# A convolution by FFT in front of two feed-forward layers: filter tiles loaded in pairs and unfolded on ScalarE

## The chip, the cores and the metric

The kernel runs on one core of one Trainium2 chip. The metric is the device time of one execution in microseconds (us). A core has five engines that run side by side, each through its own list of instructions in order: TensorE (PE in the profile, its weight loads PEld), VectorE (DVE), ScalarE (ACT), GpSimd (POOL) and SyncE (SP), which only issues transfers. They wait for one another by semaphores.

## What is computed

The input x has 2 batches of 3008 rows and 256 columns. Each column is convolved with a filter by way of the Fourier transform, and the result goes through two feed-forward layers with 2048 hidden units:

```python
X = np.fft.rfft(x, axis=1)
Y = X * (filt_r + 1j * filt_i)[None, :, :]
x = np.fft.irfft(Y, n=x.shape[1], axis=1).reshape(B * S, D)
h = x @ moe_w_in
x = np.where(h > 0.0, h, np.exp(np.minimum(h, 0.0)) - 1.0) @ moe_w_out
h = x @ moe2_w_in
return (h * np.clip(h + 3.0, 0.0, 6.0) / 6.0) @ moe2_w_out
```

## The kernel before

The transform of 3008 points is split into 47 times 64. A batch is handled in two halves of 128 columns (h is 0 or 1). For each half the opening runs these stages, which the string `PROLOGUE` (line 865) names by letters, with the half and a number behind:

- S1 (`s1t`, line 154): the 47-point transforms, seven pieces of up to 5 rows. For half 0 they run before the string starts; the letter A is that stage for half 1. Each piece fills a PSUM bank and is copied into the tile `zt`, in turn by ScalarE and VectorE.
- T (`tr`, line 170): four transposes of `zt` into a bank and a copy of it into SBUF: by ScalarE for g 0, 2, 3, 4, 5, by VectorE for g 1. The first T of a half needs all seven copies of S1.
- S (`s2_mm` and `mult`, lines 210 and 217): the 64-point transforms of group g (6 groups in a half), then the product with the filter: VectorE makes two products of 64 partitions (the imaginary part, with the halves of the partitions exchanged) and one of 128 (the real part), GpSimd adds them.
- I (`i2_mm`, `i2_evac`): the inverse 64-point transform, a copy by ScalarE and a store to a scratch in DRAM (`scr2`) that regroups the rows.
- V and O (`v_load`, `i1_mm`, `i1_evac`): the scratch is loaded again and the inverse 47-point transforms run. V for a half needs all six stores of the half.

The filter tile of half h and group g holds on its 128 partitions the 64 frequencies twice over (the host doubles them, line 1196), the real part and the imaginary part side by side. `f_load` (line 142) loads one tile of 512 KB, `f_sign` (line 146; the letter F) multiplies its imaginary part on GpSimd by a sign table `sg`. There are 12 such tiles for batch 0, all loaded at the start, and 12 again for batch 1 much later (lines 993 and 994).

`LOADS` (line 872) gives the order in which SyncE issues the first transfers: F is a filter tile, X a quarter of the input of half 1, W the raw weights, M a matrix. The other letters of `PROLOGUE`: c and k take one step of the conversion of weights into two parts (`w_chain`, line 383 on), B runs S1 for batch 1, X splits a block for the first layer, G and H run the first matmuls of the first layer (`g1_half`, `g1`), x and w load input and weights. After the string, the loop over `units` (line 1095) runs the first layer, two or three steps of weight conversion beside each unit.

The order is written out by hand: inside `tc.manual_schedule()` every engine runs its instructions in the order in which the program makes them, and semaphores are put in from the data. PSUM has seven banks in a rotating pool (`bank`, line 55) and one alone; tiles of 4 KB per partition come from a pool of 21 (`t4`, line 53).

Of the kernel before, what the change touches and what calls it, by code (L numbers as in the profile page):

```python
# [9 lines left out]
F32 = mybir.dt.float32  # L10
# [13 lines left out]
P = 128  # L24
# [23 lines left out]
def fft_conv_moe_moe2(ctx, tc, xp, fq, sg, cs1, cs1t, cs2, ci2, ci1, ident, w1i, w1o, w2i, w2o, out):  # L48
# [16 lines left out]
    def t4(shape, dt=F32):  # L65
        return p4.tile(shape, dt, tag="t4", name=name("t4"))
# [10 lines left out]
    def evac(eng, dst, src):  # L77
        if eng is nc.scalar:
            nc.scalar.activation(dst, src, AF.Copy)
        else:  # L80
            eng.tensor_copy(dst, src)  # L81
# [10 lines left out]
    def flat(t):  # L92
        return t.rearrange("p k d -> p (k d)")
# [19 lines left out]
    def load_mat(key, src, queue=nc.scalar):  # L113
        k, m = src.shape
        mats[key] = const.tile([k, m], F32, name=key)
        queue.dma_start(mats[key], src)
# [19 lines left out]
    def x_load(b, h, q):  # L136
        xin[b, h, q] = t4([P, 8, P])
        n = 4 if (b, h, q) == (0, 0, 0) else 8
        for j in range(0, 8, n):
            nc.sync.dma_start(xin[b, h, q][:KP, j : j + n], xp[b, h, :, 8 * q + j : 8 * q + j + n, :])  # L140

    def f_load(b, h, g):
        filt[b, h, g] = t4([P, 2, 4, P])
        nc.sync.dma_start(filt[b, h, g], fq[h, g])

    def f_sign(b, h, g):
        fi = filt[b, h, g][:, 1, :, :]
        s = mats["sg"][:, 4 * g : 4 * g + 4].unsqueeze(2).broadcast_to([P, 4, P])
        nc.gpsimd.tensor_tensor(out=fi, in0=fi, in1=s, op=ALU.mult)


    zt = {}

    def s1t(b, h, jg, eng):
# [60 lines left out]
            mm3(accs[h, g], *mats["s2r"], *map(pairs, parts), True, True)  # L215

    def mult(b, h, g):
        f = filt.pop((b, h, g))
        acc, parted = accs.pop((h, g)), lambda t: t
        if b:  # L220
            acc, parted = sorted_(acc), halves_of
        u, v = t2([P, 512]), t2([P, 512])
        for c in range(2):
            a, o = slice(64 * c, 64 * c + 64), slice(64 - 64 * c, 128 - 64 * c)
            nc.vector.tensor_tensor(out=parted(v[o]), in0=acc[a], in1=parted(flat(f[a, 1])), op=ALU.mult)
        nc.vector.tensor_tensor(out=parted(u), in0=acc, in1=parted(flat(f[:, 0])), op=ALU.mult)
        ws[b, h, g] = t2([P, 512])
        nc.gpsimd.tensor_tensor(out=ws[b, h, g], in0=u, in1=v, op=ALU.add)  # L228

# [45 lines left out]
    def w_raw(layer, f):  # L275
        wi, wo = ((w1i, w1o), (w2i, w2o))[layer]
        raw = p4.tile([P, 512, 2], U32, tag="t4", name=name("raw"))
        nc.sync.dma_start(
            raw[:, 0:256, :].rearrange("p (c f) t -> p c (f t)", c=2),
            wi.bitcast(U32)[:, f * 2 * P : (f + 1) * 2 * P].rearrange("(c p) f -> p c f", p=P),  # L280
        )
        nc.sync.dma_start(
            raw[:, 256:512, :].rearrange("p f t -> p (f t)"),
            wo.bitcast(U32)[f * P : (f + 1) * P, :],
        )
        raws[layer, f] = raw
# [566 lines left out]
    def fetch1(f):  # L853
# [9 lines left out]


    PROLOGUE = """
        T00 T01 T02 S00 T03 F01 S01 T04 F01 S02 T05 F01 S03 I00 F01 S04 I01 F01 A10 A11 F01 S05
        I02 A12 A13 A14 I03 c01 F01 A15 A16 c01 I04 T10 c01 T11 I05 F01 T12 w00 x00 S10 T13 S11
        T14 F01 S12 T15 S13 V00 I10 F01 S14 I11 S15 k01 B00 I12 O00 I13 O01 I14 o02 c01 I15 c01
        c01 k01 c01 x01 O03 X00 X01 O04 V10 k01 O05 k01 k01 w01 O06 B01 G00 X02 G01 k01 B02 B03
        O10 o11 o12 G02 X10 X11 O13 k01 o14 X12 k01 k01 k01 H00 O15 k01 H01 k01 H02 O16  # L870
    """
    LOADS = [(0, None, q, None) for q in range(4)]
    for x in "F00 F01 F02 F03 X0 X1 X2 X3 F04 F05 F10 W0 M F11 F12 F13 F14 F15".split():
        if x == "M":
            LOADS.append((None, None, None, None))
        elif x[0] == "F":
            LOADS.append((int(x[1]), int(x[2]), None, None))
        elif x[0] == "W":
            LOADS.append((None, None, None, int(x[1:])))
        else:  # L880
            LOADS.append((1, None, int(x[1:]), None))
    conv = w_chain(WLEAD, NF, fetch1, True)
    n_steps = 7 * (NF - WLEAD) - 12
    span = NI * (NF - 1) - 1
# [137 lines left out]
        i1(1, jg, T + 43 + max(0, jg - 1))  # L1022

    with tc.manual_schedule():
        for key, src in (("s1t", cs1t), ("id", ident), ("sg", sg), ("s2", cs2), ("i2", ci2), ("i1", ci1)):
            load_mat(key, src)
        three = const.tile([P, 1], F32, name="three")
        nc.vector.memset(three, 3.0)
        engs = (nc.scalar, nc.vector)

        acc = bank()
        for n in WARM:
            zeros = (nc.const_aps.tensor(0.0, [P, k], F32) for k in (P, n))
            nc.tensor.matmul(acc[:, :n], *zeros, start=True, stop=True)  # L1034
        for h, g, q, r in LOADS:
            if q is not None:
                x_load(0, h, q)
            elif g is not None:
                f_load(0, h, g)
            elif r is not None:  # L1040
                w_raw(0, r)
            else:
                load_mat("s1", cs1, nc.sync)
        for jg in range(JG):
            s1t(0, 0, jg, engs[jg % 2])
        lead = w_chain(0, WLEAD, lambda f: None)
        f_sign(0, 0, 0)
        f_sign(0, 0, 1)
        nsign = 2
        for step in PROLOGUE.split():  # L1050
            what, h, g = step[:-2], int(step[-2]), int(step[-1])
            if what == "T":
                tr(0, h, g, nc.scalar if g > 1 else engs[g])
            elif what == "S":
                s2_mm(0, h, g)
                mult(0, h, g)
            elif what == "A":
                s1t(0, h, g, engs[g % 2])
            elif what == "I":
                i2_mm(0, h, g)  # L1060
                i2_evac(0, h, g)
            elif what == "V":
                for q in range(4):
                    v_load(0, h, q)
            elif what == "O":
                i1_mm(0, h, g)
                i1_evac(0, h, g, nc.scalar)
            elif what == "o":
                i1_mm(0, h, g)
                i1_evac(0, h, g, nc.vector)  # L1070
            elif what == "k":
                steps(conv, g)
            elif what == "c":
                steps(lead, g)
            elif what == "X":
                x_split(0, g, h)
            elif what == "F":
                for _ in range(g):
                    f_sign(0, *divmod(nsign, 6))
                    nsign += 1  # L1080
            elif what == "x":
                x_load(1, h, g)
            elif what == "w":
                w_raw(0, WLEAD + g)
            elif what == "B":
                s1_plain(h, g)
                s1_evac(1, h, g, True)
            elif what == "G":
                g1_half(units[g], 0)
            elif what == "H":  # L1090
                g1(units[g])
                if g:
                    g_split(units[g - 1])

        for n, u in enumerate(units):
            place[0] = n
            for fn in pre[n]:
                fn()
            if n >= NI:
                g1(u)  # L1100
                g_split(units[n - 1])
            if n >= SKEW:
                g2(units[n - SKEW])
            for fn in post[n]:
                fn()
        def rest(n):
            def run():
                if n == NU:
                    g_split(units[-1])
                g2(units[n - SKEW])  # L1110
                for fn in post[n]:
                    fn()
            return run

        old = None
        n = place[0] = NU
        for l, p in ROUNDS:
            for q in range(GROUPS):
                old = group(l, p, q, old, [rest(NU + i) for i in range(3)], pre[n : n + 4])
                n += 4  # L1120
        prod(old.l, old.p, old.q, 3, old.c, False)
        old.high((1, 1))
        old.gate((1, 0))
        old.add((0, 1), old.u2, old.c)
        old.low((1, 1))
        old.high((1, 0))
        old.relu((0, 1))
        old.low((1, 0))
        old.gate((0, 1))
        old.high((0, 1))  # L1130
        old.low((0, 1))
        for key in ((0, 0), (1, 1), (1, 0), (0, 1)):
            old.second(key)
            if key == (1, 0):
                out_evac(old.l, old.p, 0)
        out_evac(old.l, old.p, 1, True)
# [82 lines left out]
```

## Time and profile before

| | before |
|---|---|
| median of 3 runs | 1045.99 us (1045.93 to 1046.16) |
| the profiled execution | 1045.9 us |
| its span in the trace | 1044.0 us |
| TensorE busy | 1037.5 us, 99% of the span |
| VectorE busy | 873.3 us, 84% |
| ScalarE busy | 805.8 us, 77% |
| GpSimd busy | 194.7 us, 19% |
| granted TensorE clock over the span | 1.00 |

The profile gives each engine's busy time as a share of the span. The 1.9 us between the span and the execution's time lie outside what the trace covers. TensorE's matmuls are pipelined and their ends are modelled, so its busy share hides short gaps; these are better read from the starts of its instructions.

### The profile page before, as it was taken

Reading aid. Unit: us, or ns where it says so; the run is one execution under the profiler, and the core shown is the slowest. Engines: PE = TensorE matmul, PEld = TensorE weight load, DVE = VectorE, ACT = ScalarE, POOL = GpSimd, SP = SyncE. Lnnn points to the kernel's source line nnn. Section 1 sums busy time; section 2 is a strip of 40 time slices with the busy share of each in tenths; the row PEclk is TensorE's granted clock in tenths of the full one; section 3 lists DMA queues with packets and bytes.
Section 4 is the critical chain, followed back from the end, with each engine's and each line's share of the span. In section 5 each row is a group of like instructions: output and inputs, shape, how many; then the busy total and the mean of one; then the engine's idle time right before and its main releaser. Section 6 shows DMA issues by size and latency. Waiting matters only on the chain.

```text
span 1044.0 us, 14383 instructions
## 1 busy us (share of the span) xinstructions
PE 1037.5 (99%) x5018; PEld 913.5 (88%) x5018; DVE 873.3 (84%) x1412; ACT 805.8 (77%) x1448; POOL 194.7 (19%) x212
## 2 busy tenths in 40 slices
PE   9999999999999999999999999999999999999998
PEld 6688888888899989988888888888888888888998
DVE  4889999888877788799898988888888888887776
ACT  3488888897778888888988877777777777777775
POOL 3700002455447735000111000010010010000000
PEclk9999999999999999999999999999999999999999
DMA  9992100475546534330385432100100100100101
GB/s 285 327 306 82 31 1 1 152 235 178 173 124 216 198 125 154 127 102 11 124 291 144 153 126 82 41 21 21 41 21 21 41 18 19 40 1 1 41 1 36
DMA packets 58056, 107.31 MB, mean 103 GB/s; under 512 B 5024, under 2 KB 33696, under 8 KB 57984
## 3 DMA queue, kind: packets, MB, share of 16 engines
q1 hardware_dynamic: 52112, 88.16, 25.4%
q0 software_dynamic: 4896, 17.83, 5.6%
q8 instruction: 39, 0.64, 0.3%
q10 hardware_dynamic: 976, 0.41, 0.2%
q14 instruction: 33, 0.27, 0.1%
HBM read 69.42 MB, written 36.96 MB: 102 GB/s over the span
## 4 chain that ended last, share of the span: by engine, by line
PE 97%; ACT 1%; DVE 1%; POOL 0%; issue 0%; DVEq 0%; ACTq 0%; POOLq 0%
PE ps L88 27%; PE ps L89 27%; PE ps L90 27%; PE lone L88 3%; PE lone L90 3%; PE lone L89 3%; PE ps L256 2%; PE ps L160 1%; PE ps L233 1%; PE ps L213 1%; PE ps L1034 0%; PE ps L173 0%; POOL t L228 0%; PE ps L184 0%; DVE t L85 0%
## 5 line engine op out<-in xcount | busy, mean ns | idle before, releaser
L88 PE MATMUL ps<-t,w 128*128 128x512 f32 (+1 forms) x1072 | 403.4, 376 | 0.7 <-DVE t L509 0.7
L89 PE MATMUL ps<-t,w 128*128 128x512 f32 (+1 forms) x1072 | 401.5, 375 | 0.0
L90 PE MATMUL ps<-t,w 128*128 128x512 f32 (+1 forms) x1072 | 401.4, 374 | 0.0
L88 PEld LDWEIGHTS ps<-t,w 128*128 128x128 f32 x1072 | 202.6, 189 | 25.5 <-DVE t L509 1.7
L89 PEld LDWEIGHTS ps<-t,w 128*128 128x128 f32 x1072 | 202.6, 189 | 24.7 <-DVE w L327 1.2
L90 PEld LDWEIGHTS ps<-t,w 128*128 128x128 f32 x1072 | 202.6, 189 | 24.0 <-DVE t L701 0.2
L701 DVE TENSOR_TENSOR t<-t,t 128x512 fp32r<-128x512 f32 (+1 forms) x256 | 175.6, 699 | 24.3 <-ACT t L696 22.7
L696 ACT ACTIVATE t<-t 128x512 fp32r<-128x512 f32 (+1 forms) x256 | 154.2, 616 | 6.0 <-DVE t L686 5.7
L650 ACT ACTIVATE t<-ps 128x512 f32<-128x512 f32 (+1 forms) x175 | 102.6, 586 | 60.6 <-PE ps L90 58.9
L670 ACT ACTIVATE t<-t,three 128x512 f32<-128x512 f32 (+1 forms) x143 | 96.5, 707 | 38.0 <-DVE t L656 37.2
L686 DVE SCALAR_TENSOR_TENSOR t<-t,t 128x512 f32<-128x512 f32 (+1 forms) x143 | 97.0, 705 | 33.3 <-ACT t L670 32.8
L506 ACT ACTIVATE t<-ps 128x512 f32<-128x512 f32 (+1 forms) x128 | 74.3, 581 | 45.1 <-PE ps L90 36.3
L656 DVE TENSOR_TENSOR t<-ps,t 128x512 f32<-128x512 f32 (+1 forms) x128 | 86.7, 678 | 11.4 <-ACT t L650 10.8
L507 ACT ACTIVATE t<-t 128x512 f32<-128x512 f32 (+1 forms) x128 | 79.3, 619 | 4.1
L509 DVE SCALAR_TENSOR_TENSOR ps<-t,ps 128x512 f32<-128x512 f32 (+1 forms) x76 | 50.4, 664 | 30.3 <-ACT t L507 29.6
L85 DVE TENSOR_TENSOR t<-t,t 128x512 fp32r<-128x512 f32 (+2 forms) x92 | 66.7, 730 | 3.7 <-ACT t L84 3.5
L84 ACT ACTIVATE t<-t 128x512 fp32r<-128x512 f32 (+2 forms) x104 | 62.8, 616 | 1.8 <-DVE t L81 1.3
L570 POOL TENSOR_TENSOR t<-t,t 128x512 f32<-128x512 f32 (+1 forms) x12 | 16.3, 1359 | 243.5 <-DVE t L656 214.4
L90 PE MATMUL ps<-t,t 128*128 128x512 f32 (+1 forms) x160 | 60.1, 376 | 0.0
L89 PE MATMUL ps<-t,t 128*128 128x512 f32 (+1 forms) x160 | 60.1, 376 | 0.0
L88 PE MATMUL ps<-t,t 128*128 128x512 f32 (+1 forms) x160 | 60.1, 376 | 0.0
L90 PE MATMUL lone<-t,w 128*128 128x512 f32 (+1 forms) x144 | 54.0, 375 | 0.0
(121 smaller groups left out, 1607.7 us busy)
## 6 DMA issues: line engine op xcount, KB each, us to landing
t<-in_fq SPq DMA_DIRECT2D x24, 512.0 KB, 6.2
scrw<-t SPq DMA_DIRECT2D x16, 512.0 KB, 3.0
w<-scrw POOLq DMA_DIRECT2D x16, 512.0 KB, 4.3
scr<-t SPq DMA_DIRECT2D x24, 256.0 KB, 3.3
t<-scr SPq DMA_DIRECT2D x16, 384.0 KB, 5.9
t<-in_xp SPq DMA_DIRECT2D x15, 384.0 KB, 6.2
scrx<-t SPq DMA_DIRECT2D x10, 512.0 KB, 3.1
t<-scr POOLq DMA_DIRECT2D x10, 512.0 KB, 4.8
```

Of the source, the lines that this page charges most:

```text
L85: eng.tensor_tensor(out=lo, in0=src, in1=_f32(hi), op=ALU.subtract)
L88: nc.tensor.matmul(acc, wh, xh, start=start, stop=False, skip_group_check=more)
L89: nc.tensor.matmul(acc, wl, xh, start=False, stop=False, skip_group_check=more)
L90: nc.tensor.matmul(acc, wh, xl, start=False, stop=stop, skip_group_check=more)
L506: nc.scalar.activation(r, acc, AF.Relu, scale=-1.0)
L507: nc.scalar.activation(t[:, :n], t[:, :n], AF.Exp, scale=-1.0)
L650: nc.scalar.activation(like(t, self.n), got(bank_, self.n), AF.Copy)
L656: nc.vector.tensor_tensor(out=like(self.h[key], n), in0=got(bank_, n), in1=like(u, n), op=ALU.add)
L670: nc.scalar.activation(like(r, n), h, AF.Relu, bias=three)
L686: stt(out=r, in0=r, scalar=6.0, in1=h, op0=ALU.min, op1=ALU.mult)
L696: nc.scalar.activation(gh[:, : self.n], g[:, : self.n], AF.Copy)
L701: nc.vector.tensor_tensor(out=gl[:, :n], in0=g[:, :n], in1=_f32(gh[:, :n]), op=ALU.subtract)
```

## The change

Two neighbouring groups of a half (2r and 2r + 1) share one transfer: the upper 64 partitions of the one and the lower 64 of the next lie side by side in DRAM, so 512 KB hold both filters once. `p_load` (the letter P in `LOADS`) issues it into a tile t. `f_even` (the letter d in `PROLOGUE`) puts the signs on both with one GpSimd instruction and has ScalarE make three copies of 64 partitions by 512 columns into a second tile u; after it group 2r can be used. `f_odd` (the letter e) makes two more copies, after which group 2r + 1 can be used. `mult` takes its halves from t and u accordingly. Further: the copies of S1 for half 1 (A) are all on ScalarE; the matrices `i2` and `i1` are loaded by SyncE's queue among the first loads, not by ScalarE's; a second sign table `pairsg` is made by two small GpSimd copies; `LOADS` and `PROLOGUE` have a new order. Batch 1 keeps `f_load` and `f_sign`.

```diff
+    def p_load(h, r):
+        filt[0, h, 2 * r] = t4([P, 2, 4, P])
+        rows = fq.rearrange("h g p c k d -> (h g p) (c k d)")
+        first = (6 * h + 2 * r) * P
+        nc.sync.dma_start(
+            filt[0, h, 2 * r].rearrange("p c k d -> p (c k d)"), rows[first + 64 : first + 64 + P]
+        )
+
+    lower, upper = slice(0, 64), slice(64, P)
+
+    def f_even(h, r):
+        t, u = filt[0, h, 2 * r], t4([P, 2, 4, P])
+        filt[0, h, 2 * r + 1] = u
+        nc.gpsimd.tensor_tensor(
+            out=t[:, 1], in0=t[:, 1],
+            in1=mats["pairsg"][:, r].unsqueeze(2).broadcast_to([P, 4, P]), op=ALU.mult,
+        )
+        evac(nc.scalar, u[lower, 0], t[lower, 0])
+        evac(nc.scalar, u[upper, 0], t[lower, 0])
+        nc.scalar.activation(u[upper, 1], t[lower, 1], AF.Copy, scale=-1.0)
+
+    def f_odd(h, r):
+        t, u = (filt[0, h, 2 * r + i] for i in range(2))
+        evac(nc.scalar, t[lower, 0], t[upper, 0])
+        nc.scalar.activation(u[lower, 1], t[upper, 1], AF.Copy, scale=-1.0)
@@ def mult(b, h, g):
-        f = filt.pop((b, h, g))
+        if b:
+            real = filt.pop((b, h, g))
+            imag = real, real
+        else:
+            t, u = (filt[b, h, g // 2 * 2 + i] for i in range(2))
+            real = t if g % 2 else u
+            imag = (u, t) if g % 2 else (t, u)
...
-            nc.vector.tensor_tensor(out=parted(v[o]), in0=acc[a], in1=parted(flat(f[a, 1])), op=ALU.mult)
-        nc.vector.tensor_tensor(out=parted(u), in0=acc, in1=parted(flat(f[:, 0])), op=ALU.mult)
+            nc.vector.tensor_tensor(out=parted(v[o]), in0=acc[a], in1=parted(flat(imag[c][a, 1])), op=ALU.mult)
+        nc.vector.tensor_tensor(out=parted(u), in0=acc, in1=parted(flat(real[:, 0])), op=ALU.mult)
@@ the order of the opening
-        T00 T01 T02 S00 T03 F01 S01 T04 F01 S02 T05 F01 S03 I00 F01 S04 I01 F01 A10 A11 F01 S05
-        I02 A12 A13 A14 I03 c01 F01 A15 A16 c01 I04 T10 c01 T11 I05 F01 T12 w00 x00 S10 T13 S11
-        T14 F01 S12 T15 S13 V00 I10 F01 S14 I11 S15 k01 B00 I12 O00 I13 O01 I14 o02 c01 I15 c01
-        c01 k01 c01 x01 O03 X00 X01 O04 V10 k01 O05 k01 k01 w01 O06 B01 G00 X02 G01 k01 B02 B03
-        O10 o11 o12 G02 X10 X11 O13 k01 o14 X12 k01 k01 k01 H00 O15 k01 H01 k01 H02 O16
+        x00 T00 d00 e00 T01 T02 T03 d01 S00 T04 S01 T05 c01 A10 A11 e01 x01 d02 S02 I00 c01 e02
+        w00 A12 d10 S03 I01 S04 I02 S05 A13 A14 I03 A15 A16 I04 c01 I05 w01 T10 e10 c01 c01 T11
+        d11 T12 S10 S11 V00 T13 T14 T15 k01 e11 B00 d12 S12 e12 S13 S14 I10 S15 I11 O00 I12 k01
+        I13 O01 I14 c01 X00 o02 I15 c01 B01 B02 k01 k01 X01 O03 k01 X02 k01 O04 k01 G00 k01 G01
+        k01 O05 G02 V10 k01 O06 k01 B03 k01 O10 o11 o12 k01 X10 X11 O13 o14 X12 H00 O15 H01 H02
+        O16
-    for x in "F00 F01 F02 F03 X0 X1 X2 X3 F04 F05 F10 W0 M F11 F12 F13 F14 F15".split():
+    LOADS = "P00 X0 i2 P01 W0 X1 P02 i1 X2 X3 P10 P11 P12 M".split()
@@ before the opening
-        for key, src in (("s1t", cs1t), ("id", ident), ("sg", sg), ("s2", cs2), ("i2", ci2), ("i1", ci1)):
+        for key, src in (("s1t", cs1t), ("id", ident), ("sg", sg), ("s2", cs2)):
             load_mat(key, src)
+        mats["pairsg"] = const.tile([P, 3, 4], F32, name="pairsg")
+        for i, half in enumerate((lower, upper)):
+            signs = mats["sg"].rearrange("p (r i k) -> p i r k", r=3, i=2)
+            nc.gpsimd.tensor_copy(mats["pairsg"][half], signs[half, i])
...
-        f_sign(0, 0, 0)
-        f_sign(0, 0, 1)
...
-                s1t(0, h, g, engs[g % 2])
+                s1t(0, h, g, nc.scalar)
```

## Rows read from the trace of the kernel before

**Rows 1.** The page's first part: engine, busy us (share of span), instructions.
```profile
PE 1037.5 (99%) x5018; PEld 913.5 (88%) x5018; DVE 873.3 (84%) x1412; ACT 805.8 (77%) x1448; POOL 194.7 (19%) x212
```

**Rows 2.** TensorE in order of time: start, us, instruction, count [idle before, releaser].
```profile
20.02 1.02 PE L233 MATMUL ps<-t,i 128*128 128x512 f32 x2
20.88 1.02 PE L213 MATMUL ps<-t,s 128*128 128x512 f32 x2
22.12 1.12 PE L233 MATMUL ps<-t,i 128*128 128x512 f32 x2 [0.21 <-POOL t L228]
...
33.81 1.04 PE L173 MATMUL ps<-id,zt 128*128 128x128 f32 x8
...
41.62 1.02 PE L213 MATMUL ps<-t,s 128*128 128x512 f32 x2
42.80 1.12 PE L233 MATMUL ps<-t,i 128*128 128x512 f32 x2 [0.16 <-POOL t L228]
...
51.64 1.13 PE L233 MATMUL ps<-t,i 128*128 128x512 f32 x2
...
56.83 0.78 PE L88 MATMUL ps<-t,w 128*128 128x512 f32 x1
57.45 0.38 PE L89 MATMUL ps<-t,w 128*128 128x512 f32 x1
57.67 0.38 PE L90 MATMUL ps<-t,w 128*128 128x512 f32 x1
...
59.82 0.59 PE L184 MATMUL ps<-t,s 96*96 96x512 f32 x1
60.55 3.56 PE L256 MATMUL ps<-i,t 96*128 96x94 f32 x30
...
71.88 0.38 PE L89 MATMUL lone<-t,w 128*128 128x512 f32 x1
72.28 0.48 PE L90 MATMUL lone<-t,w 128*128 128x512 f32 x1
72.60 0.38 PE L88 MATMUL ps<-t,w 128*128 128x512 f32 x1
...
78.21 0.38 PE L90 MATMUL ps<-t,w 128*128 128x512 f32 x1
79.32 0.48 PE L88 MATMUL ps<-t,w 128*128 128x512 f32 x1 [0.73 <-DVE t L509]
```

**Rows 3.** Busy us of each engine by stretch, then clock, DMA share and GB/s.
```profile
20.00:30.00 10.00, 9.79 (x57) 6.97 (x57) 8.63 (x13) 3.04 (x5) 9.30 (x9) 1.00 1.03 368
30.00:40.00 10.00, 10.00 (x57) 6.89 (x57) 8.04 (x13) 5.54 (x10) 5.62 (x6) 1.00 1.01 331
```

**Rows 4.** ScalarE in order of time, in the opening.
```profile
14.52 0.60 ACT L79 ACTIVATE t<-ps 128x512 f32<-128x512 f32 x1 [0.74 <-PE ps L173]
...
44.03 0.60 ACT L243 ACTIVATE t<-ps 128x512 f32<-128x512 f32 x1 [1.60 <-PE ps L233]
44.52 0.66 ACT L306 ACTIVATE t<-raw 128x512 f32<-128x512 f32 x1
...
54.40 1.15 ACT L84 ACTIVATE t<-t 128x512 fp32r<-128x512 f32 x2
```

**Rows 5.** VectorE in order of time: the products with the filters.
```profile
39.23 1.39 DVE L225 TENSOR_TENSOR t<-ps,t 64x512 f32<-64x512 f32 x2
...
41.37 1.39 DVE L225 TENSOR_TENSOR t<-ps,t 64x512 f32<-64x512 f32 x2
```

**Rows 6.** GpSimd in order of time: a sign and an addition.
```profile
19.80 1.04 POOL L149 TENSOR_TENSOR t<-t,sg 128x512 f32<-128x512 f32 x1
20.80 1.26 POOL L228 TENSOR_TENSOR t<-t,t 128x512 f32<-128x512 f32 x1
```

**Rows 7.** ScalarE in order of time, as the loop over units begins.
```profile
73.71 0.89 ACT L306 ACTIVATE t<-raw 128x512 f32<-128x512 f32 x1
74.51 0.58 ACT L506 ACTIVATE t<-ps 128x512 f32<-128x512 f32 x1
```

More of the change, by code (lines that the diff above doesn't have):

```diff
@@ L865, in fft_conv_moe_moe2 @@
     PROLOGUE = """
-        T00 T01 T02 S00 T03 F01 S01 T04 F01 S02 T05 F01 S03 I00 F01 S04 I01 F01 A10 A11 F01 S05
-        I02 A12 A13 A14 I03 c01 F01 A15 A16 c01 I04 T10 c01 T11 I05 F01 T12 w00 x00 S10 T13 S11
-        T14 F01 S12 T15 S13 V00 I10 F01 S14 I11 S15 k01 B00 I12 O00 I13 O01 I14 o02 c01 I15 c01
-        c01 k01 c01 x01 O03 X00 X01 O04 V10 k01 O05 k01 k01 w01 O06 B01 G00 X02 G01 k01 B02 B03
-        O10 o11 o12 G02 X10 X11 O13 k01 o14 X12 k01 k01 k01 H00 O15 k01 H01 k01 H02 O16
-    """
-    LOADS = [(0, None, q, None) for q in range(4)]
-    for x in "F00 F01 F02 F03 X0 X1 X2 X3 F04 F05 F10 W0 M F11 F12 F13 F14 F15".split():
[L874 to L881, printed above, removed]
+        x00 T00 d00 e00 T01 T02 T03 d01 S00 T04 S01 T05 c01 A10 A11 e01 x01 d02 S02 I00 c01 e02
[4 more added lines that the diff above has]
+        O16
+    """
+    LOADS = "P00 X0 i2 P01 W0 X1 P02 i1 X2 X3 P10 P11 P12 M".split()
     conv = w_chain(WLEAD, NF, fetch1, True)
@@ L1034, in fft_conv_moe_moe2 @@
             nc.tensor.matmul(acc[:, :n], *zeros, start=True, stop=True)
[L1035 to L1041, printed above, removed]
+        for q in range(4):
+            x_load(0, 0, q)
+        for x in LOADS:
+            n = int(x[-1]) if x[1:] else 0
+            if x[0] == "P":
+                p_load(int(x[1]), n)
+            elif x[0] == "X":
+                x_load(0, 1, n)
+            elif x[0] == "W":
+                w_raw(0, n)
+            elif x[0] == "i":
+                load_mat(x, {"i1": ci1, "i2": ci2}[x], nc.sync)
             else:
@@ L1046, in fft_conv_moe_moe2 @@
         lead = w_chain(0, WLEAD, lambda f: None)
-        f_sign(0, 0, 0)
-        f_sign(0, 0, 1)
-        nsign = 2
         for step in PROLOGUE.split():
@@ L1076, in fft_conv_moe_moe2 @@
                 x_split(0, g, h)
[L1077 to L1080, printed above, removed]
+            elif what == "d":
+                f_even(h, g)
+            elif what == "e":
+                f_odd(h, g)
             elif what == "x":
```

## The prediction

> **What bounds the kernel now.** I read the busy times first: TensorE is busy 1037.5 of 1044.0 us [rows 1]. The reader is to see that no edit of the opening can win more than the gaps of TensorE there; the matmuls themselves are the same before and after, only their order changes. Next I read the list of TensorE's instructions in order of time and subtract starts, since modelled ends hide gaps. Where nothing is waited for, two 512-column records of an S or I step take 20.88 - 20.02 = 0.86 us, and one record of the first layer takes 57.67 - 57.45 = 0.22 [rows 2]. Against these, six places in the first 80 us are late [rows 2]:
>
> - a. 20.88 to 22.12 is 1.24 instead of 0.86: 0.38, an I step waiting for GpSimd's addition.
> - b. 41.62 to 42.80 is 1.18: 0.32, the same in half 1.
> - c. 56.83 to 57.45 is 0.62 instead of 0.22: 0.40, the first matmul of the first layer (G00).
> - d. 59.82 to 60.55 is 0.73 instead of 0.43 (half of 0.86): 0.30, the first O step of half 1, whose load V has only just landed.
> - e. 71.88 to 72.60 is 0.72 for two records instead of 0.44: 0.28.
> - f. 78.21 to 79.32 is 1.11 instead of 0.22: 0.89, a bank not yet released by VectorE.
>
> Together 2.57 us. Some single waits of about 0.1 are left uncounted, and the wait before the first T stays as it is: the code up to it is the same.
>
> **The change part by part.** *Transfers.* Six loads of 512 KB fall away, 3.1 MB. The stretches 20 to 40 move 331 to 368 GB/s with the DMA engines at a share of 1.0 [rows 3], so that is some 9 us of a full queue. None of it is on TensorE's path as long as the data lands before its turn, and in list a to f only d waits for a transfer: V of half 1 stands in SyncE's queue behind an input load that the new order issues long before. I take d as gone and nothing else for the transfers. The two matrices that SyncE's queue takes over are small and needed first by I00 and O00, both after 20 us.
>
> *GpSimd.* Twelve signs at 1.04 us become six: 6.2 us less. In a, a sign (19.80) stood in front of the addition (20.80) that the I step wanted [rows 6]. In the new order no sign stands between S01's addition and I01, and seven steps of TensorE (T05, A10, A11, S02, I00, A12, S03) lie between S01 and I01. Gone: a. In half 1, S11, T13, T14, T15, B00, S12, S13 and S14 stand between S10 and I10. Gone: b. The signs for later pairs wait for their transfers in front of additions in GpSimd's list (the one for P10 in front of S03's addition), but that addition cannot run before VectorE's product, so I cost it at nothing; if P10 landed later than about 27 us, I03 would wait for it.
>
> *ScalarE.* This is the new work: five copies a pair, 30 in all, ahead of copies that TensorE needs. No row shows a copy of 64 partitions on ScalarE, nor one that changes the half. The lower bound is nothing (added work gives no time back), the upper one two passes of a whole copy, 2 x 0.62. VectorE's products give the nearest case: two of 64 partitions across the halves take 1.39, 0.69 each [rows 5], no more than the engine needs for a full tile; so I take the price of a full SBUF copy. Two of those take 1.15 us, and if one lasts 0.62, starts are 0.53 apart [rows 4]. [...]
>
> Now the sum for half 0. ScalarE starts the copy of the first T at 14.52 [rows 4], and what feeds it is unchanged. From there to the last copy of A, which the first T of half 1 needs, its list holds 9 copies from PSUM for T and I at 0.49 (44.03 to 44.52) = 4.4; 7 of A at no more than 0.60 = 4.2; 18 filter copies at 0.53 = 9.5; one step of weights, 0.66; 18.8 in all, so ready at 33.3. T10 runs at 33.81 now [rows 2]; the new order has I05 ahead of it and gap a is gone: 33.81 + 0.86 - 0.38 = 34.3. So ScalarE, which was busy 3.0 and 5.5 of 10 us there [rows 3], becomes full, with 1.0 us to spare: 0.06 for each of the 18 copies. Queued behind the copies on ScalarE are those of T, I and A; a bank comes round again after seven uses, and in the tightest place (A15 takes the bank that I01's copy frees) I make the margin a few tenths. I cost this at nothing. The remaining 12 copies lie between T10 and I10 under the same spacing, with VectorE as their taker.
>
> *VectorE* loses three copies of A and waits no more for signs. In half 1 its six products follow each other at 41.37 - 39.23 = 2.14 [rows 5]: S10 now starts at about 34.3 + 1.4 for three T, ends 0.86 later at 36.6, so the last product ends at 36.6 + 12.8 = 49.4, and the addition (1.26 [rows 6]) at 50.7. I15 starts at 51.64 now and, without a and b, would at 50.9 [rows 2]. That is nearly a tie; I put 0.2 us on the path for it.
>
> *Order at the end of the opening.* G00 now comes after B01, B02, O03 and O04, so its parts are long there: c is gone. All 13 k steps lie before X10; before, five of the 12 lay around H00 to H02. That matters for e and f: at 73.71 a weight step on ScalarE takes 74.51 - 73.71 = 0.80 us in front of the relu of the next unit [rows 7], and VectorE has four such steps among the first gates. With these done earlier, in time in which VectorE had been idle, I take e and f as gone.
>
> The sum: 2.57 - 0.2 = 2.4 us less. The profiled execution took 1045.9, its span 1044.0, the median is 1045.99; from 1045.9 this gives **1043.5 us**. If a few small waits go too and the tie is won, 1042.6; if f stays in part, 1044.2.
>
> **The rivals.** *Copies at their full duration.* If filter copies don't overlap, each costs 0.62, 0.09 more. That is 1.6 for 18, less the 1.0 to spare: 0.6 at T10; and 1.1 for the other 12, of which perhaps 0.2 shows: 1043.5 + 0.8 = 1044.3. [...] Against: 1.15 for two copies.
>
> *The gain is given back among the units.* If f comes from VectorE being full from there on and not from the steps in its way, e and f (1.17) return: 1044.7. For it: VectorE is busy 84% of the span [rows 1], more in this stretch. Against: after 79.32 TensorE runs on with hardly a gap under the same load.
>
> *Slower: copies across the halves are dear.* Place: d00 to e12 on ScalarE. With δ more per copy, the stall is 18δ - 1.0 at T10 and about 12δ - 0.9 up to I15. It eats the 2.4 at δ = 0.14 and costs 2.1 beyond that at δ = 0.21, a copy of 0.74. At the upper bound (1.24, δ = 0.71) the time is 1043.5 + 19.4 = 1062.9; near the deciding point 1046 to 1048. Against it: VectorE crosses halves at no price [rows 5].
>
> *A load that lands late.* SyncE's list is in order; a store of I waiting for ScalarE's late copy holds back everything behind it, V of half 1 above all. If the first O of half 1 waits 1 to 2 us: 1045.0.
>
> *The change doesn't do what it says:* no; both the number of transfers and the order are written out.
>
> **How the numbers follow.** The forecast has 0.56 (its own range 1042.6 to 1044.2), full-duration copies 0.16, the units 0.11, dear copies 0.10, a late load 0.07. A measurement of this kernel can tell about 0.2%, 2.1 us, from no change, so faster means under 1043.9: 0.49 of the forecast's 0.56 and 0.03 of the others, 0.52. Slower: dear copies for the most part and 0.02 of others, 0.11. The rest, 0.37, is the same. The range goes from 1042.6 to 1046.2, which leaves out the worse half of the dear copies and little else.
>
> **What would show it.** In the changed kernel's trace: filter copies 0.53 apart on ScalarE; ScalarE near 10 of 10 from 15 to 34 us; T10 at about 34.3 and no gap of 0.2 or more before it; I01, I10, G00 and the first O of half 1 without a wait; no 0.9 gap among the first units. T10 later than 35, or TensorE waiting for ScalarE's copies between 20 and 45, would make it wrong; so would VectorE still releasing banks late after 70.

## The result and the profile after

The changed kernel is slower: median 1053.29 us of 20 runs (1046.07 to 1059.86) against 1046.08 of 20 runs of the kernel before. The ratio is 1.0054, 95% interval 1.0039 to 1.0069; it is not that of the two medians, which would be 1.0069. Forecast were 1043.5, and 1042.6 to 1046.2 as the range. The times lie in two groups that the granted clock tells apart: eight executions with a mean clock of 0.999 or 1.000 took 1046.07 to 1048.69 us, twelve with 0.987 to 0.993 took 1051.28 to 1059.86. So even with a full clock the changed kernel doesn't gain: the middle of the eight is 1047.8. The kernel before has two executions out of 20 at 1050.7 and 1051.0; in its runs beside the experiments below, such times come with a mean clock of 0.995. The profiled execution is the fastest of the twelve: 1051.28 us, span 1049.5, clock 0.993.

The page of the changed kernel, busy times and the clock in 40 slices:

```profile
PE 1042.8 (99%) x5018; PEld 919.2 (88%) x5018; DVE 875.9 (83%) x1409; ACT 822.4 (78%) x1481; POOL 189.0 (18%) x208
...
PEclk9979999999999999999999999999999999999999
```

The clock of the kernel before:

```profile
PEclk9999999999999999999999999999999999999999
```

TensorE is as busy as before by share [rows 1]; ScalarE has 16.6 us more, GpSimd 5.7 less. New is the third digit of the clock: a 7 at 52 to 79 us, where the kernel before had nines throughout. The stretches show it (columns as in [rows 3]; the first two lines are to be held against the two lines there):

```profile
20.00:30.00 10.00, 9.92 (x46) 5.93 (x44) 9.22 (x13) 9.83 (x19) 7.16 (x6) 1.00 1.02 321
30.00:40.00 10.00, 9.88 (x51) 6.58 (x52) 8.56 (x12) 9.55 (x20) 4.09 (x4) 1.00 0.83 235
...
60.00:70.00 10.00, 9.00 (x49) 9.03 (x50) 3.12 (x7) 4.56 (x9) 0.00 (x0) 0.63 1.04 336
70.00:80.00 10.00, 10.00 (x42) 8.85 (x42) 4.95 (x10) 6.42 (x13) 0.00 (x0) 0.69 0.96 316
```

From 60 to 80 the clock is 0.63 and 0.69. In steps of half a microsecond it is 1.00 up to 62.5, then 0.53, then 0.50 in every step from 63.0 to 76.0, then 0.81, and 1.00 again from 76.5. Half clock for 7.4 and 6.2 us gives the two means, 13.6 us together. TensorE in order of time, against [rows 2]:

```profile
12.77 1.97 PE L199 MATMUL ps<-id,zt 128*128 128x128 f32 x16 [0.42 <-ACT zt L79]
...
28.87 1.05 PE L265 MATMUL ps<-t,i 128*128 128x512 f32 x2
30.12 1.80 PE L186 MATMUL ps<-s1t,t 96*128 96x96 f32 x14 [0.20 <-ACT t L275]
...
34.89 1.98 PE L239 MATMUL ps<-t,s 128*128 128x512 f32 x4
...
50.48 1.13 PE L265 MATMUL ps<-t,i 128*128 128x512 f32 x2
...
55.31 0.46 PE L88 MATMUL ps<-t,w 128*128 128x512 f32 x1
55.61 0.38 PE L89 MATMUL ps<-t,w 128*128 128x512 f32 x1
...
58.87 1.03 PE L210 MATMUL ps<-t,s 96*96 96x512 f32 x2
61.00 9.55 PE L288 MATMUL ps<-i,t 96*128 96x94 f32 x50 [1.10 <-DMA t<-scr]
...
76.65 0.46 PE L88 MATMUL ps<-t,w 128*128 128x512 f32 x1
```

At 61.00 the first O step of half 1 has waited 1.10 us for its load V. Behind that wait, 1.5 us after the step's start, the clock falls: 50 records of O, which with a full clock take 5.5 us (e1 below), take 70.26 - 61.00 = 9.3 us. To compare stages, three more rows of the kernel before, the first T, S10 and the first matmul behind the string `PROLOGUE`:

```profile
13.82 1.53 PE L173 MATMUL ps<-id,zt 128*128 128x128 f32 x12 [0.42 <-ACT zt L79]
...
35.98 1.02 PE L213 MATMUL ps<-t,s 128*128 128x512 f32 x2
...
70.29 0.46 PE L88 MATMUL ps<-t,w 128*128 128x512 f32 x1
```

| stage, us | before | after | difference |
|---|---|---|---|
| start to first T | 13.82 | 12.77 | -1.05 |
| first T to S10 | 22.16 | 22.12 | -0.04 |
| S10 to I15 | 15.66 | 15.59 | -0.07 |
| I15 to the first O of half 1 (after: with G02, 0.65) | 8.91 | 10.52 | +1.61 |
| from there to the end of the string (after: without G02) | 9.74 | 15.65 | +5.91 |
| the rest of the span | 973.71 | 972.85 | -0.86 |
| sum | 1044.0 | 1049.5 | +5.5 |

The first line is no gain of the change: the first matmuls of this execution ran faster (S1's 64 in 7.28 us, 7.79 before), and in e6, whose program has the same matmuls up to there, the first T starts at 13.97. So in this execution the loss has one place, the load V of half 1 and the clock behind it. That is not all of it in the others: eight have the full clock and still no gain, and the first stage, which ran without a wait here, is taken up under e6. SyncE's queue shows what stood ahead of V, the store of B01 and the raw weights number 4:

```profile
53.12 0.32 SPq L227 DMA_DIRECT2D scr<-t  x1
53.53 0.39 SPq L310 DMA_DIRECT2D raw<-in_w1i  x1
53.98 0.80 SPq L314 DMA_DIRECT2D raw<-in_w1o  x1
55.33 4.04 SPq L280 DMA_DIRECT2D t<-scr  x4
```

The first O step reads the first of the four loads V. It was issued 55.33 - 50.48 = 4.85 us behind the start of I15 and took 5.5 us to land; in the kernel before these are 4.43 and 4.4.

### The profile page after: what moved, and what is told of

Its sections match the earlier page's. It is cut to its first block, busy times and chain, and to the rows that moved or that the text cites. A ratio compares the mean times of both kernels' runs of the same rounds, so it can differ in the third digit from the quotient of the medians.

```text
span 1049.5 us, 14402 instructions
## 1 busy us (share of the span) xinstructions
PE 1042.8 (99%) x5018; PEld 919.2 (88%) x5018; DVE 875.9 (83%) x1409; ACT 822.4 (78%) x1481; POOL 189.0 (18%) x208
## 4 chain that ended last, share of the span: by engine, by line
PE 97%; DVE 1%; ACT 1%; DMA 1%; issue 0%; DVEq 0%; ACTq 0%
PE ps L88 27%; PE ps L90 27%; PE ps L89 27%; PE ps L288 3%; PE lone L88 3%; PE lone L89 3%; PE lone L90 3%; PE ps L186 1%; PE ps L239 1%; PE ps L265 1%; DMA t<-scr 1%; PE ps L199 1%; PE ps L1062 0%; PE ps L210 0%; DVE t L85 0%
```

## The experiments

Theory A: these transfers delay V, TensorE waits, and the clock falls behind the wait. Theory B: ScalarE's filter copies are at fault. Theory C: what is short is a free tile buffer. Three more came with the second set. Theory D: with `i2` and `i1` on SyncE's queue, the first stage gets its input late. Theory E: VectorE's products set the time from S10 to I15. Theory F, against E: ScalarE's copies or the PSUM banks set it.

**e1: the raw weights behind V.** The new letter `r00` issues `w_raw(0, 4)`.

```diff
-        if f + 2 < NF:
+        if f + 2 < NF and f != 2:
...
-        k01 O05 G02 V10 k01 O06 ...
+        k01 O05 G02 V10 r00 k01 O06 ...
```

> The changed kernel with one transfer moved: the raw weights number 4 (two loads of 256 KB), which stand in SyncE's queue just ahead of the loads V of half 1, are issued behind them. Theory A (the loads V of half 1 land late behind these weights, the first O step of half 1 waits 1.1 us for them, and the granted clock falls behind that wait): the wait at about 60 us shrinks below 0.3 us, the clock stays at 1.00 through 60 to 80 us in nearly all executions, and the median falls from 1053 to 1043.5 to 1045. Theory B (the filter copies on ScalarE make TensorE patchy between 14 and 50 us and the clock falls for that, whatever V does): still half clock for some 13 us in most executions, 1050 to 1055. Theory C (what waits at 60 us is not the transfer but a free tile buffer): the wait stays at about 1 us, since the number of tiles in use falls by one only.

Measured: 1046.44 us, 12 runs; 1.0021 of before (1.0008 to 1.0035). Seven executions with a clock of 0.999 or more took 1045.56 to 1046.57. Two more at 0.998 took 1047.9 and 1048.8. The profiled one is among three at 1051.8 to 1052.2, and it lost its clock elsewhere, behind a wait in the first stage. At the disputed place nothing waits: the O step starts 0.86 us behind the record ahead of it, in the changed kernel 61.00 - 58.87 = 2.13 (TensorE, then the stretch):

```profile
66.85 1.03 PE L210 MATMUL ps<-t,s 96*96 96x512 f32 x2
67.71 5.72 PE L288 MATMUL ps<-i,t 96*128 96x94 f32 x50
...
60.00:70.00 10.00, 10.00 (x70) 8.48 (x69) 8.08 (x16) 7.24 (x18) 0.00 (x0) 1.00 0.85 214
```

Moving these two loads takes 6.9 us off the median. B falls for this place: the copies are all there, and the clock is full. A and C are not told apart by e1 alone, since the raw weights also take a tile of the pool that V's loads use. In the changed kernel SyncE waited 0.6 us for an O step to release a tile ahead of the first load V, and that load was issued 0.6 us later behind I15 than in e1 (4.21); it also took 5.5 us to land instead of 4.5. So up to 0.6 us of the delay may be C's; e2 shows the transfers alone. And 1046 is not the expected 1043.5 to 1045; e6 goes on from here. The wait of the first stage, and the stretch behind it:

```profile
8.47 10.05 PE L186 MATMUL ps<-s1t,t 96*128 96x96 f32 x48 [0.92 <-DMA t<-in_xp]
...
10.00:20.00 10.00, 9.58 (x45) 9.34 (x45) 1.31 (x2) 1.58 (x3) 2.08 (x2) 0.50 1.05 251
```

**e2: the kernel before, with raw weights ahead of V.**

```diff
-        ... O04 V10 k01 O05 k01 k01 w01 O06 ...
+        ... O04 w01 V10 k01 O05 k01 k01 O06 ...
```

> The kernel before with one step moved: the raw weights of w01 are issued ahead of the loads V of half 1 instead of behind them; nothing else is changed, no filter pairs. Theory A: the first O step of half 1 waits for V 1 to 2 us longer than before (0.3 us), and in part of the executions the granted clock falls to half behind it, so that the median is 1047 to 1054 and the times spread over some 8 us. Theory B: the wait alone costs what it lasts, 1047 to 1048, and the clock stays at 1.00.

Measured: 1053.96 us, 12 runs (1046.88 to 1055.36); 1.0054 (1.0034 to 1.0075). Eight executions ran at 0.991 to 0.993 and took 1053.3 to 1055.4, four at 1.000 and took 1046.9 to 1047.6. No filter pair, no new order, the same loss. The first load V is issued 4.42 us behind I15, as before (4.43), and takes 6.1 us to land instead of 4.4: here the delay is the transfers' alone. The first O, and the stretch behind it:

```profile
63.06 5.90 PE L256 MATMUL ps<-i,t 96*128 96x94 f32 x30 [1.73 <-DMA t<-scr]
...
70.00:80.00 10.00, 10.00 (x40) 9.19 (x40) 5.22 (x11) 4.21 (x10) 0.00 (x0) 0.50 1.02 350
```

**e4: the new order with whole tiles.** Each P issues two `f_load`, d and e are one `f_sign` each, `mult` as before.

```diff
-                p_load(int(x[1]), n)
+                for g in (2 * n, 2 * n + 1):
+                    f_load(0, int(x[1]), g)
...
-            elif what == "d":
-                f_even(h, g)
-            elif what == "e":
-                f_odd(h, g)
+            elif what in "de":
+                f_sign(0, h, 2 * g + (what == "e"))
```

> The changed kernel with the filters of batch 0 loaded as twelve whole tiles and signed by GpSimd one by one as before (each P issues two loads, each d and e is one sign): the new order and the A copies on ScalarE without the pairs and without the filter copies. Theory A: 3.1 MB more stand in the queue, about 8 us, but they have long landed at 55 us, so that the wait for V of half 1 stays at about 1 us and the clock falls as often as in the changed kernel: 1047 to 1055, unless additions wait for signs early on. Theory B (the filter copies are at fault): the clock stays at 1.00 and the time is 1044 to 1046.

Measured: 1058.66 us, 6 runs (five at 1052.81 to 1061.14, and one at 1070.8 that the ratio leaves out); 1.0113 (1.0092 to 1.0133). Worse than either theory said, since I had taken the 3.1 MB for hidden. What TensorE waited for in the first 90 us (total, times, longest):

```profile
PE ps L186 <- DMA t<-in_xp: 4.3, 2, 4.0
PE ps L288 <- DVE t L258: 3.7, 1, 3.7
PE ps L288 <- DMA t<-scr: 1.0, 1, 1.0
```

The A steps wait 4.0 us for the input of half 1, which stands behind whole filter tiles. The 3.7 us are the first O step of half 0: its first load V, issued at 51.13, took 4.3 us to land, and the step starts at 55.55. So the new order needs the halved transfers. The wait for V of half 1 is there too, 0.98 us at 73.52, and here the clock stays:

```profile
70.00:80.00 10.00, 9.02 (x70) 8.03 (x69) 6.27 (x15) 5.47 (x12) 0.00 (x0) 1.00 1.03 303
```

**e5: the pairs in the old order.** `p_load` in place of every second F of `LOADS`; in place of the signs, in turn, `f_even` and `f_odd`:

```diff
-                    f_sign(0, *divmod(nsign, 6))
+                    (f_odd if nsign % 2 else f_even)(nsign // 6, nsign % 6 // 2)
```

> The kernel before with the pairs alone: half the filter transfers, one sign and five ScalarE copies a pair, put where the signs stood; the old order otherwise, A copies in turn on ScalarE and VectorE. Theory A: V of half 1 stays behind only what it was behind before, so no wait over 0.5 us at 60 us and a full clock; TensorE waits up to 1 us more between 14 and 45 us because ScalarE's copies stand in front of T's at places not made for them: 1045.5 to 1047. Theory B: patchy TensorE and half clock in many executions, over 1050.

Measured: 1053.69 us, 5 runs (1052.41 to 1054.01); 1.0074 (1.0062 to 1.0086), at clocks of 0.997 to 1.000. Again missed: not up to 1 us of waits on ScalarE but 7.0, of which 0.4, ahead of the first T, is in the kernel before as well:

```profile
PE ps L240 <- ACT t L79: 4.1, 3, 1.8
PE ps L200 <- ACT zt L79: 2.9, 2, 2.5
```

The copies cost what stands behind them: ahead of the first T's copy they hold up TensorE at once; in the new order they don't. Pairs and order only work together.

**e6: as e1, the matrices back on ScalarE's queue.**

```diff
-        for key, src in (("s1t", cs1t), ("id", ident), ("sg", sg), ("s2", cs2)):
+        for key, src in (("s1t", cs1t), ("id", ident), ("sg", sg), ("s2", cs2), ("i2", ci2), ("i1", ci1)):
...
-    LOADS = "P00 X0 i2 P01 W0 X1 P02 i1 X2 X3 P10 P11 P12 M".split()
+    LOADS = "P00 X0 P01 W0 X1 P02 X2 X3 P10 P11 P12 M".split()
```

> The kernel of e1_raw4_behind_V10 with the two matrices i2 and i1 loaded from ScalarE's queue again, as before, so that the third quarter of the input is again issued at about 4 us and not at 2.1. Open is why e1 with a full clock takes 1046.1 and not about 1044.8. Theory D (the earlier issue of the third quarter makes the second one land late, 8.4 us against 6.8, so that the first stage waits up to 1 us, and in some executions loses the clock there): the second quarter lands by 7.2 us, the median falls to 1044.5 to 1045.2, and half clock near 9 us becomes rare. Rival (how fast the first transfers run varies from execution to execution whatever their order): no change against e1, 1046.0 to 1046.6, and waits of up to 1 us in the first stage remain.

Measured: 1044.87 us, 12 runs (1044.12 to 1046.25); 0.9984 of before (0.9974 to 0.9995), all with a clock of 0.999 or more. This beats both kernels, by 1.1 us the one before. TensorE, from S10 to the end of the string:

```profile
36.08 1.98 PE L239 MATMUL ps<-t,s 128*128 128x512 f32 x4
...
51.66 1.13 PE L265 MATMUL ps<-t,i 128*128 128x512 f32 x2
...
60.05 1.02 PE L210 MATMUL ps<-t,s 96*96 96x512 f32 x2
60.92 5.72 PE L288 MATMUL ps<-i,t 96*128 96x94 f32 x50
...
69.92 0.46 PE L88 MATMUL ps<-t,w 128*128 128x512 f32 x1
```

**e7: the kernel before, the matrices on SyncE's queue.** The same two transfers the other way, alone: `i2` and `i1` issued behind the first quarter of half 1's input.

> The kernel before with one thing changed: the matrices i2 and i1 are loaded from SyncE's queue behind the first quarter of half 1 instead of from ScalarE's queue at the start. Theory D (with two transfers fewer in front, SyncE issues the third quarter of the input 2 us earlier, and the second quarter, which TensorE wants first, lands later): the first stage waits for its input, the median rises by 0.8 to 1.3 us, to 1046.7 to 1047.2, and some executions fall to half clock near 9 us. Rival (between e1 and e6 the difference of 1.2 us has another source, such as i2 and i1 landing between the filters): within 0.3 us of before.

Measured: 1046.90 us, 12 runs (1045.45 to 1050.93), against 1045.75 of the kernel before beside it: the medians differ by 1.15, as expected (0.8 to 1.3), but the ratio is 1.0007 (0.9995 to 1.0019), which doesn't exclude none. Its profiled execution has no wait in the first stage. That the place of the two matrices costs some 1 us beside the filter pairs is shown by e1 and e6 (their intervals don't meet, and of the executions with a clock of 0.999 or more e1's middle is 1046.06, e6's 1044.87); that it does so by a late second quarter of the input is seen in e1's trace alone and stays open.

**e14: the changed kernel, the matrices on ScalarE's queue.** The edit of e6 without that of e1.

> The changed kernel with the matrices i2 and i1 on ScalarE's queue again and the raw weights 4 left ahead of the loads V of half 1. Theory A with D: the first stage is that of before, but the first O step of half 1 still waits 1 to 1.5 us for V, and more than half of the executions run 13 to 17 us at half clock behind it: two groups of times, about 1046 and about 1053. Rival (the wait at 60 us follows from the late start alone): no wait, 1044.9 as e6.

Measured: 1051.90 us, 12 runs; 1.0047 (1.0026 to 1.0068). Three executions at a full clock, 1045.4 to 1046.3; nine at 0.990 to 0.993, 1051.5 to 1054.8. The three lie below or at the edge of the changed kernel's eight at a full clock (1046.07 to 1048.69), which agrees with e6 on the matrices. As expected, the wait is there again, with the clock behind it:

```profile
PE ps L288 <- DMA t<-scr: 1.1, 1, 1.1
...
60.00:70.00 10.00, 8.86 (x48) 8.31 (x47) 3.74 (x8) 4.52 (x10) 0.00 (x0) 0.67 1.05 319
```

**e11: V right behind the store of I15** (as e6; raw weights 4 behind B03).

```diff
-        ... o02 I15 c01 B01 B02 ...
+        ... o02 I15 c01 V10 B01 B02 ...
...
-        k01 O05 G02 V10 r00 k01 O06 k01 B03 k01 ...
+        k01 O05 G02 k01 O06 k01 B03 r00 k01 ...
```

> The kernel of e6 with the loads V of half 1 issued right behind the store of I15, ahead of B01's store, and raw weights 4 behind B03. In e1 the first of these loads landed 0.5 us before the first O step of half 1 wanted it. Theory A: it now lands 2 us or more before, so that no execution waits there: the spread narrows, half clock after 60 us does not occur, and the median is that of e6's full-clock executions or lower, 1044.3 to 1045.2, faster than before by 0.05 to 0.15%. Rival C (free tile buffers): moving them earlier takes buffers that B02, X01 and O03 want, and ScalarE's copies of O steps wait instead: the same or later than e6.

Measured: 1054.75 us, 6 runs (1054.17 to 1055.17); 1.0076 (1.0058 to 1.0094), all at 0.992 or 0.993. The expected 1044.3 to 1045.2 is missed; rival C named what happened. V is in time, the first O step of half 1 starts at 60.61 without a wait, and the next ones wait instead. ScalarE, then TensorE:

```profile
64.42 0.61 ACT L79 ACTIVATE t<-ps 128x260 f32<-128x260 f32 x2 [5.22 <-DMA scr<-t]
...
64.86 3.51 PE L288 MATMUL ps<-i,t 96*128 96x94 f32 x15 [3.00 <-ACT t L79]
```

ScalarE's copy of O05 waits 5.2 us for a store to end, B01's, which now runs behind the four loads V and holds the buffer that the copy wants; TensorE waits 3.0 us for the bank, and every execution has lost clock.

**e9: short products in half 1.** VectorE's real product of batch 0, half 1 is left out, as e6 otherwise.

```diff
-        nc.vector.tensor_tensor(out=parted(u), in0=acc, in1=parted(flat(real[:, 0])), op=ALU.mult)
+        if b or not h:
+            nc.vector.tensor_tensor(out=parted(u), in0=acc, in1=parted(flat(real[:, 0])), op=ALU.mult)
+        else:
+            u = v
```

> The kernel of e6 with VectorE's third product of half 1 of batch 0 left out (the real part is not computed, GpSimd adds the imaginary part to itself): 6 times 0.75 us less on VectorE between S10 and I15. Theory E (the time from S10 to I15, 15.6 us before and after the change alike, is set by VectorE's six products in a row, which is why removing GpSimd's signs won nothing there): the waits of 0.1 to 0.14 us at I12 to I15 vanish, S10 to I15 takes 14.8 us and the time falls by 0.6 to 0.9 against e6. Rival F (ScalarE's copies or the PSUM banks set it): S10 to I15 stays at 15.4 or more, the time within 0.3 of e6.

Measured: 1043.89 us, 10 runs; 0.9979 (0.9966 to 0.9991), 1.0 below e6. S10 to I15:

```profile
35.52 1.98 PE L239 MATMUL ps<-t,s 128*128 128x512 f32 x4
...
50.56 1.05 PE L268 MATMUL ps<-t,i 128*128 128x512 f32 x2
```

50.56 - 35.52 = 15.04, against 15.58 in e6 and 15.66 before: the stage is shorter by 0.54, and the waits at its I steps are gone. I expected 14.8. The rest of the 1.0 lies elsewhere: in e9's trace the first T starts 0.56 us earlier than in e6's, at 13.41, where the two kernels have the same code.

**e10: no filter copies.** As e6, the 30 copies left out; both groups of a pair read the tile t as it was loaded and signed.

```diff
-        evac(nc.scalar, u[lower, 0], t[lower, 0])
-        evac(nc.scalar, u[upper, 0], t[lower, 0])
-        nc.scalar.activation(u[upper, 1], t[lower, 1], AF.Copy, scale=-1.0)
...
-        evac(nc.scalar, t[lower, 0], t[upper, 0])
-        nc.scalar.activation(u[lower, 1], t[upper, 1], AF.Copy, scale=-1.0)
```

> The kernel of e6 with all 30 ScalarE copies of the filters left out (the products read the pair's tile as it was loaded, so half of the filter values are wrong; the signs stay): about 16 us less on ScalarE. Theory E: ScalarE was nearly full but only the wait for a bank at A15 (0.4 us) came from it, VectorE sets the rest: 0.3 to 0.8 us less than e6. Rival F: the copies set the pace of the opening: 1.5 us or more less than e6, 1043.5 or below with a full clock.

Measured: 1044.60 us, 10 runs; 0.9981 (0.9969 to 0.9992), 0.3 below e6, with intervals that lie on each other. The expected 0.3 to 0.8 is met at its lower end; F, which asked for 1.5 or more, falls. The copies cost little in the new order. S10 to I15 stays, at 15.50:

```profile
36.21 1.98 PE L234 MATMUL ps<-t,s 128*128 128x512 f32 x4
...
51.71 1.12 PE L260 MATMUL ps<-t,i 128*128 128x512 f32 x2
```

## Why the prediction was wrong, point by point

**Gap d and the late load: the step that failed.** I took the wait of 0.30 at the first O of half 1 for gone because an input load no longer stands ahead of V. I looked at what had left SyncE's queue ahead of V, not at what had come: with nine k steps ahead of V instead of two, the eighth, which issues the raw weights number 4, comes before it, and the store of B01 too. The wait became 1.10 us. e1 takes it away with the raw weights, B01's store left where it is. The rival "a load that lands late" named the queue, gave it 0.07 and 1045.0, and put it on a late store of I; it is the right place with the wrong transfer.

**The clock: not in the prediction at all.** Every case priced a wait of TensorE at its length. In the profiled execution the wait is followed by some 13.6 us at a clock of 0.50, and 12 of 20 executions of the changed kernel have lost about as much clock or more (0.987 to 0.993 over the span). They lie 6.7 us above the other eight, middle against middle (1054.5 and 1047.8), which is most of the miss. e2 brings it about in the kernel before by moving one step, and e1 removes it from this place.

**The two matrices: put at nothing, and wrongly.** I called them small and needed late, and took the code up to the first T as the same; the loads ahead of it were not. Back on ScalarE's queue they give 1.6 us of the median (e1 to e6), 1.2 at a full clock. Where they are, seven of the eight executions of the changed kernel at a full clock lie above the range too. By which transfer they do it stays open (e7).

**Gaps a and b: right in the row, wrong in the sum.** In the changed kernel the first I of each half no longer waits for GpSimd, yet S10 to I15 takes 15.59 instead of 15.66, not 0.32 less. VectorE's products run without a pause:

```profile
36.11 1.41 DVE L257 TENSOR_TENSOR t<-ps,t 64x512 f32<-64x512 f32 x2 [0.79 <-PE ps L239]
...
46.88 1.39 DVE L257 TENSOR_TENSOR t<-ps,t 64x512 f32<-64x512 f32 x2
48.28 0.69 DVE L258 TENSOR_TENSOR t<-ps,t 128x512 f32<-128x512 f32 x1
```

From the start of the first to the end of the last they take 49.0 - 36.1 = 12.9 us, and GpSimd's addition stands behind them; the working of the prediction had 12.8. I called that a tie with TensorE and put 0.2 on it. It was the bound: the waits that b had held came back as smaller ones at later I steps (ahead of I14 ten records of O take 48.30 - 47.11 = 1.19, in e9 1.09), and they go when VectorE has less to do (e9, 0.54 us). That the same products were the bound in the kernel before is argued from the equal times, not tried. In half 0 the new wait for a bank at A15 (28.87 to 30.12, 1.25 instead of 0.86: 0.39) took the place of gap a; I had left it "a few tenths" of margin. e10 has no copies and still needs 22.1 from the first T to S10, by a wait of 0.30 for an addition; there VectorE is likely the bound too, but that wasn't tried.

**ScalarE: the price nearly right.** The nearest row was the right one, VectorE's that crosses the halves at no price (0.69 for 64 partitions, 0.69 for the full tile at 48.28 above). A whole copy of 0.62, as the forecast had it, is in this line of the kernel before; ScalarE's copies in the changed kernel are in the lines below it:

```profile
53.30 0.62 ACT L323 ACTIVATE w<-t 128x512 fp32r<-128x512 f32 x1
```

```profile
13.96 1.26 ACT L79 ACTIVATE t<-t 64x512 f32<-64x512 f32 x2
15.13 0.61 ACT L171 ACTIVATE t<-t 64x512 f32<-64x512 f32 x1
15.77 0.63 ACT L79 ACTIVATE t<-t 64x512 f32<-64x512 f32 x1
16.30 0.61 ACT L176 ACTIVATE t<-t 64x512 f32<-64x512 f32 x1
16.82 1.05 ACT L79 ACTIVATE t<-ps 128x512 f32<-128x512 f32 x2
```

Five starts in 16.82 - 13.96 = 2.86, 0.57 each, where the sum had 0.53; each lasts 0.61 to 0.63. ScalarE is full from 20 to 40 (9.83 and 9.55), as forecast. TensorE waited 0.39 us for it at A15, which the prediction had named as a sign that it was wrong; T10 still starts 33.55 - 12.77 = 20.8 us behind the first T, where 20.5 was forecast. The rival of dear copies falls by the spacing and by e10, 0.3 us for all 30. The rival of copies at full duration (0.8 us) is not told apart by the times, whose intervals overlap; the spacing lies between it and the forecast.

**Transfers: priced at nothing, rightly only with the new order.** e4 shows that the order without the halved transfers loses 4.0 us at A and 3.7 at the first O step; the saving is what the order lives on, not a spare.

**Gaps c, e and f.** c is gone (55.31 to 55.61, 0.30, of which 0.08 is over the 0.22). e and f were to give 1.17: the rest of the span, from the end of the string, is 0.86 shorter in the changed kernel and 1043.1 - 69.92 = 973.2, 0.5 shorter, in e6. There f is still 78.53 - 77.68 = 0.85 instead of 0.22, so 0.63 of its 0.89. So about half.

**What is left of the sum.** In e6, where neither the late V nor the matrices disturb, the span is 0.9 below that of before and the median 1.1, not 2.4: c, d, e and f in part, next to nothing from a and b.

## What to carry to other kernels

When an order is changed, read for each load on the critical path which transfers now stand ahead of it in its queue, and which buffers they and it wait for; a step list that computes may also issue. A wait that several producers end in turn is not won back by making one of them faster: follow the longest chain through the stage (here six products of VectorE) before counting gaps. And price a new wait of TensorE of a microsecond not at its length alone, but at what the granted clock did behind such waits in that kernel.

## What the hardware showed that I had not expected

- In the profiled executions a wait of TensorE was followed by a stretch at a lower clock: 1.10 us in the changed kernel (0.50 from 63.0 to 76.0), 1.14 in e14 (0.67 as the mean of 60 to 70), 1.73 in e2 and 3.00 in e11 (0.50 from 70 to 80 in both). In the changed kernel the engine was busy in all of 50 to 80 us but that wait (9.90, 9.00 and 10.00 of 10 us). By their mean clock, 12 of 20 executions of the changed kernel have lost clock, 9 of 12 of e14, 8 of 12 of e2 and 6 of 6 of e11; where in them isn't traced. The groups with and without the loss lie 6.7 us apart in the changed kernel, 7.0 in e14 and 7.4 in e2 (middle against middle), several times the wait.
- A wait of about 1 us doesn't decide it. In e4 one of 0.98 us at the same O step left the clock at 1.00, and so did gap f (0.89) in the kernel before; in e1 one of 0.92 in the first stage was followed by half clock (0.50 from 10 to 20 us). What decides is not shown.
- The first transfers differ from one execution to the next: TensorE's first stage waited 0.92 us in e1's profiled execution and not at all in that of the changed kernel, which has the same first transfers.
